# Single blocks at the opening of two passes, a moved product, and one tile in another PSUM bank, in a two-layer decode kernel with its gradients

## The chip, the cores and the metric

The kernel runs on one core of one Trainium2 chip. The metric is the device time of one execution in microseconds (us); the number of a kernel is the median of its runs. Lower is better.

## The reference

One token (S = 1, D = 1024) goes through four blocks: attention over a cache of 65536 positions (32 query heads, 4 groups of cached heads, 128 wide), a feed-forward block (3584 wide, squared ReLU), then the same two with the same weights again. The outputs are the result and the gradients of it (for a given grad_out) by x, both caches, and all weights and biases.

```
def A(x, k_cache, v_cache, wq, wo):          # caches: (1, 4, 65536, 128)
    q = (x @ wq) as (32 heads, 128); k, v repeated 8 times over the heads
    p = softmax(q k^T * 128**-0.5)
    return (p v) @ wo
def B(x, w1, b1, w2, b2):
    return relu(x @ w1 + b1)**2 @ w2 + b2
x = x + A(layernorm(x));  x = x + B(layernorm(x))
x = x + A(layernorm(x));  x = x + B(layernorm(x))
out, vjp = jax.vjp(...);  return out, *vjp(grad_out)
```

All tensors are bfloat16. Each cache is 64 MB; the gradients of the caches are as large.

## The kernel before

The caches don't fit on the chip, so they are streamed from memory four times. Pass 1 is the first attention forward, pass 2 the second attention forward, pass 3 the backward pass of the second attention as far as the gradient of q (attn_bwd3), pass 4 the rest of both backward passes with the cache gradients (attn_bwd4). Between them stand dense stages for the weights. In the code the passes are p = 0 to 3.

**Items and blocks.** A pass walks over 256 items. An item is eight columns of 128 positions of one group; 64 items are a group, four items are a block (1 MB of K or V; 64 blocks of each). Each item runs through some stages with fixed lags: in pass 2 the transpose of K (kT, lag 0), the scores (kS, 2) and the V products (v8, 36); in pass 3 the transpose of V (vT, 0), the products with dO (vS, 2) and the products with K (k8, 13). After the stages of a step, a background queue does one step of work for another group: in pass 2 the query of the next group (g_q, reads wq), in pass 3 its dO and its row sums of dO o (g_dO, reads wo). These generators count steps, with some steps in which they only wait for their load. bg.need(g) finishes what is left of them before the group's first item. by_group says at which step they begin: the second group's at n // 4 = 16 of 64, the others as far into the group before theirs.

**Granules.** The arena holds 20 granules of 1 MB. Eight of them become planes that keep the softmax numerators of two layers, so in pass 3 twelve are left for everything that streams. kv8 loads a block on first touch: either a pair of blocks in two adjacent granules (take_pair; one request of 2 MB, line 370), or a single one (Slot; 1 MB, line 365). The set KV["halves"] names the blocks that are always loaded singly: the last eight of the order in which the pass touches its blocks, and at the beginning of passes 2 to 4 the first ten. Pass 4 never loads pairs (NOW["pairs"] is false there). take_pair chooses the pair whose later granule came free first, take_one the granule that has been free longest, both by the count of steps at which the plan gives granules back, not by measured time. Some blocks are kept from one pass to the next: eight K blocks into pass 2, seven V blocks into pass 3, most of them already transposed in place.

**Order.** In passes 1 to 3 and in the second dense stage the order of instructions on TensorE, VectorE and ScalarE is the order of the program (manual_schedule). In pass 4 it is made by the framework's scheduler. All loads are issued on SyncE, in program order; SyncE waits only for the granule of the load at its head, so it runs ahead of the computation. Stores are issued on GpSimd.

**The row sums.** The gradient of the scores needs dO v^T minus the row sums of dO o. Its accumulator ps_dp holds 64 columns x 8 heads (pass 3; a unit of eight items) or 32 x 16 (pass 4; a block). The unit begins with one product of the constant sel2 with ndt, the negated row sums (as two bfloat16 parts) spread to the unit's width; it starts the accumulation and writes all of it. Then come 64 (32) products of V blocks with the padded dO (dOpad, DOB). ndt is made on VectorE in vS at the group's first item, after dO_finish, right behind dOpad.

**The second dense stage.** Between passes 2 and 3 the feed-forward block runs forward and backward over w1 in seven chunks. Per chunk: ch_fwd (32 products and two VectorE steps, giving dhb), ch_bwd of the chunk before, ch_spread (four products spread dhb over the partitions, ScalarE copies them to wvb), ch_turn (four groups of transposes of w1; ScalarE copies three of them, VectorE one) and ch_dots (VectorE products of w1 with wvb). The PSUM tiles of ch_spread and of ch_turn come from one ring of three buffers, ps_tr. The tag acc has one buffer; passes 2 and 3 accumulate their outputs there.

Of the kernel before, what the change touches and what calls it, by code (L numbers as in the profile page):

```python
# [11 lines left out]
F32 = mybir.dt.float32  # L12
# [4 lines left out]
P = 128  # L17
# [3 lines left out]
def kernel(  # L21
# [35 lines left out]
    J = 32  # L57
# [3 lines left out]
    HB = 64  # L61
# [3 lines left out]
    R2, R4 = 2 * R, 4 * R  # L65
# [16 lines left out]
    PS = {}  # L82
# [5 lines left out]
    def ps_tr(shape=None, dtype=BF):  # L88
        return PS["pool"].tile(shape or [P, 8, P], dtype, name="ps_tr", tag="tr", bufs=2 if PS["pass4"] else 3)

    def ps_sc(shape, dtype=F32):
        return PS["pool"].tile(shape, dtype, name="ps_sc", tag="sc", bufs=1 if PS["pass4"] else 2)
# [4 lines left out]
    def ps_acc(shape):  # L97
        return PS["pool"].tile(shape, F32, name="ps_acc", tag="acc", bufs=1)
# [251 lines left out]
    KV = {"have": {}, "keep": set(), "halves": set(), "turn": None, "turned": set()}  # L350
# [74 lines left out]
    def start_pass(p):  # L425
        KV["keep"] = plan_keep(p)
        KV["turned"] = KV.get("next", set())
        KV["next"] = set()
        KV["turn"] = {0: "k", 2: "v"}.get(p)
        NOW["pairs"] = p < 3  # L430
        KV["halves"] = set(TOUCH[p][-8:] + (TOUCH[p][:10] if p else []))

    def f_cols(ap, nb):
        return ap[:, bass.ds(512 * (nb // 4) + nb % 4, P, step=4)]
# [342 lines left out]
    class Background:  # L777
# [35 lines left out]
        def by_group(self, p, gen):  # L813

            order = list(dict.fromkeys(g for g, _ in ITEMS[p]))
            n = len(ITEMS[p]) // G
            for k, g in enumerate(order[1:]):
                self.later.append((k * n + 8 if PS["pass4"] and k else k * n + n // 4, gen(g), g))

        def drain(self):  # L820
            while self.later:
# [376 lines left out]
    def attn_bwd3(p, L, on_group, bg, end=()):  # L1198
        st = ExitStack()
        dspool = st.enter_context(tc.tile_pool(name="b3_ds", bufs=2))  # L1200
        items = ITEMS[p]
        dOpad = vec.tile([P, G, 8, R], BF, name="dOpad")
        nc.vector.memset(dOpad[:], 0.0)
        state = {}
        gfirst = {g: next(c8 for gg, c8 in items if gg == g) for g in range(G)}
        glast = {g: [c8 for gg, c8 in items if gg == g][-1] for g in range(G)}

        def vT(g, c8):
            bg.need(g)
            vb8 = kv8("v", g, c8)  # L1210
            if is_turned("v", g, c8):
                state[("vt", g, c8)] = vb8
            else:
                pt = ps_tr()
                for i in range(8):
                    nc.tensor.transpose(pt[:, i, :], vb8[:, i, :], ident_b[:, :])  # L1216
                kv_done("v", g, c8)
                vt = turned_to("v", g, c8, vb8)
                evac(vt[:, :, :], pt[:, :, :], kind="kta" if c8 % HB // 8 in ACT_VT else "kt")
                state[("vt", g, c8)] = vt  # L1220

        def vS(g, c8):
            if c8 == gfirst[g]:
                nc.vector.tensor_copy(out=dOpad[:, g, 0, :], in_=L["dOT"][:, gsl(g)])
                ndt = dspool.tile([64, HB, R], BF, name="ndt", tag="ndt")
                nc.vector.tensor_copy(out=ndt[:, :, :], in_=L["nd2"][:, gsl(g)].unsqueeze(1).to_broadcast([64, HB, R]))
                state["ndt"] = ndt
            vt = state.pop(("vt", g, c8))
            for i in range(8):
                s = (c8 + i) % HB  # L1230
                if s == 0:
                    state["ps_dp"] = ps_sc([P, HB, R])
                    nc.tensor.matmul(state["ps_dp"][:, :, :].rearrange("p c r -> p (c r)"), lhsT=sel2[:, :],
                                     rhs=state["ndt"][:, :, :].rearrange("o c r -> o (c r)"), start=True, stop=False)
                w = min(8, HB - s)
                nc.tensor.matmul(state["ps_dp"][:, s:s + w, :].rearrange("p a b -> p (a b)"), lhsT=vt[:, i, :],
                                 rhs=dOpad[:, g, 0:w, :].rearrange("p a b -> p (a b)"), start=False, stop=(s == HB - 1))
            if is_turned("v", g, c8):
                kv_done("v", g, c8)
            if (c8 + 8) % HB == 0:  # L1240
                c0 = c8 + 8 - HB
                ps_dp = state["ps_dp"]

                def ds():
                    dsT = dspool.tile([P, HB, R], BF, name="dsT", tag="dsT")
                    nc.vector.tensor_tensor(out=dsT[:, :, :], in0=ps_dp[:, :, :], in1=E(1, g, c0, HB), op=ALU.mult)
                    add_load(dve=0.7)
                    state[("ds", g, c0 // HB)] = dsT
                after(1, ds)

        def k8(g, c8):
            kb8 = kv8("k", g, c8)
            dsT = state[("ds", g, c8 // HB)]
            if c8 % SU == 0:
                state["ps_dq"] = ps_acc([P, 8, R])
            ps_dq = state["ps_dq"]
            for i in range(8):
                c = c8 + i
                s = c % HB
                w = min(8, HB - s)  # L1260
                nc.tensor.matmul(ps_dq[:, 0:w, :].rearrange("p a b -> p (a b)"), lhsT=kb8[:, i, :],  # L1261
                                 rhs=dsT[:, s:s + w, :].rearrange("p a b -> p (a b)"),
                                 start=(c % SU == 0), stop=(c % SU == SU - 1), skip_group_check=True)
            kv_done("k", g, c8)
            if (c8 + 8) % SU == 0:
                su = c8 // SU

                def fold():
                    fold_dq(L, g, su, ps_dq[:, 0, :], gfirst[g] // SU == su, glast[g] // SU == su, dspool)
                    if glast[g] // SU == su:  # L1270
                        on_group(g)
                first_at(1, fold)

        start_pass(p)
        with tc.manual_schedule(engines=ORDERED):
            pipeline(items, [(vT, 0), (vS, TLEAD), (k8, B3_LAG)], bg, end)
        st.close()


    def attn_bwd4(p, La, Lb, on_group, bg, stack, end=()):  # L1280
# [5 lines left out]
        state = {}  # L1286
# [69 lines left out]
        def vS(g, c8):  # L1356
            if c8 == gfirst[g]:
                g_setup(g)
            vt = state.pop(("vt", g, c8))
            for i in range(8):  # L1360
                s = (c8 + i) % J
                if s == 0:
                    state["ps_dp"] = ps_sc([P, J, R2])
                    nc.tensor.matmul(state["ps_dp"][:, :, :].rearrange("p c r -> p (c r)"), lhsT=sel2[:, :],
                                     rhs=state["ndt"][:, :].unsqueeze(1).to_broadcast([64, J, R2]), start=True, stop=False)
                w = min(4, J - s)
                nc.tensor.matmul(state["ps_dp"][:, s:s + w, :].rearrange("p a b -> p (a b)"), lhsT=vt[:, i, :],  # L1367
                                 rhs=DOB[:, g, 0:w, :].rearrange("p a b -> p (a b)"), start=False, stop=(s == J - 1))
            if is_turned("v", g, c8):
                kv_done("v", g, c8)  # L1370
                if c8 % J == J - 8 and nexts:
                    NOW["newest"] = True
                    kv8(*nexts.popleft())
                    NOW["newest"] = False
                    NOW["ring"] = not nexts
            if (c8 + 8) % J == 0:
                c0 = c8 + 8 - J
                ps_dp = state["ps_dp"]
                if g == items[0][0]:
                    if c8 == J - 8 + items[0][1]:  # L1380
                        state["Xs"] = Slot("xs")
                    X = state["Xs"].t.rearrange("p (n j r) -> p n j r", j=J, r=R2)[:, c0 // J % 8, :, :]
                else:
                    X = dspool.tile([P, J, R2], BF, name="X", tag="X", bufs=3)
                nc.vector.tensor_tensor(out=split2(X[:, :, :]), in0=split2(ps_dp[:, :, :]), in1=E2(g, c0, J), op=ALU.mult)
                add_load(dve=0.13 + J * R2 * 0.00105)
                state[("X", g, c0 // J)] = X
# [310 lines left out]

    def ch_spread(s):

        pg = ps_tr([P, 512], F32)
        for j in range(4):
            nc.tensor.matmul(pg[:, j * P:(j + 1) * P], lhsT=dhb[:, 4 * s + j:4 * s + j + 1].to_broadcast([P, P]), rhs=ident_b[:, :],
                             start=True, stop=True)
        nc.scalar.copy(out=wvb[:, s % 2, :].rearrange("q (p j) -> q p j", j=4), in_=pg[:, 0:512].rearrange("q (j p) -> q p j", j=4))
# [232 lines left out]
```

## Time and profile before

| | |
|---|---|
| median of 3 runs | 1951.35 us (1949.32 to 1955.88) |
| profiled execution | 1954.17 us, span 1952.4 us |
| mean granted TensorE clock | 0.916 |
| TensorE products busy | 1592.5 us (82%) |
| VectorE busy | 1172.5 us (60%) |
| ScalarE busy | 1044.6 us (54%) |
| DMA | 787.63 MB, mean 403 GB/s |
| read from memory, written | 617.62 MB, 165.69 MB |
| K and V loads of 2 MB | 169 requests |
| K and V loads of 1 MB | 152 requests |

The profile is one execution, 1.8 us longer than its span. In it PE is TensorE, DVE VectorE, ACT ScalarE, POOL GpSimd, SP SyncE; a q behind the name (SPq) is the engine's instruction queue. L1236 is line 1236 of the kernel. A row of the timeline has start, duration, engine, line, operation, output <- input, and in brackets how long the engine had been idle and what ended that. A row of the view by stretches has the busy time of each engine with its instructions, the granted clock, the DMA share (mean busy share of 16 DMA engines; it can pass 1 a little) and GB/s. A row of waits has who waited for whom: total us, times, longest.

### The profile page before, as it was taken

The page shows a single profiled execution, that of the slowest core. Times are in us where ns is not written, and L with a number is a line of the kernel's source. Part 1 is how long each engine was busy: PE and PEld are TensorE (multiplying, and loading weights), DVE is VectorE, ACT ScalarE, POOL GpSimd, SP SyncE. Part 2 cuts the span into 40 slices and gives each one's busy share as a digit, 9 for nine tenths or more (in the row PEclk, how much of TensorE's full clock was granted, in tenths as well). Part 3 has the DMA queues.
Part 4 walks back from the last instruction along what each step waited for, and adds up shares of the span by engine and source line. Part 5 has one row for each costly group of instructions (what it writes and reads, how often), then busy time and mean ns, then how long its engine had stood idle before and what let it go on. Part 6 is the DMA issues. An engine that isn't in the chain of part 4 may idle for free. (4 is left out here: it accounts for less than half of the span.)

```text
span 1952.4 us, 66978 instructions
## 1 busy us (share of the span) xinstructions
PE 1592.5 (82%) x30199; PEld 1304.0 (67%) x30199; DVE 1172.5 (60%) x2453; ACT 1044.6 (54%) x1617; POOL 141.8 (7%) x321
## 2 busy tenths in 40 slices
PE   6878788688878888877787888889987987787977
PEld 6868778587777777777776885555554554454544
DVE  5645555255545555545464576867875886676866
ACT  3434334254334446435363455766875785676765
POOL 0000000000000000000000001211211211121211
PEclk9999899699899999999899999988996998898997
DMA  9999999999999999899999988999999999899998
GB/s 395 426 426 427 426 428 413 397 398 424 429 425 428 427 423 304 333 425 428 427 423 418 408 309 302 416 405 406 424 423 420 401 424 412 355 423 392 424 422 318
DMA packets 105997, 787.63 MB, mean 403 GB/s; under 512 B 9312, under 2 KB 16494, under 8 KB 42094
## 3 DMA queue, kind: packets, MB, share of 16 engines
q1 hardware_dynamic: 81630, 617.65, 76.8%
q0 software_dynamic: 24080, 165.70, 20.4%
q8 instruction: 236, 3.87, 0.7%
q14 instruction: 51, 0.42, 0.1%
HBM read 617.62 MB, written 165.69 MB: 401 GB/s over the span
## 5 line engine op out<-in xcount | busy, mean ns | idle before, releaser
L164 DVE COPY kt<-ps_tr 128x1024 bf16<-128x1024 bf16 x724 | 497.0, 689 | 438.2 <-PE ps_tr L1024 244.6
L161 ACT CAST arena<-ps_gg 128x1024 bf16<-128x1024 f32 x457 | 444.5, 1011 | 194.7 <-PE ps_gg L1408 145.1
L1024 PE MATMUL ps_tr<-ident_b,arena 128*128 128x128 bf16 x3840 | 309.2, 225 | 32.3 <-DMA arena<-in_A_k_cache_dram 21.0
L164 DVE CAST arena<-ps_gg 128x1024 bf16<-128x1024 f32 (+2 forms) x186 | 222.4, 1196 | 86.4 <-PE ps_gg L1408 41.6
L161 ACT COPY kt<-ps_tr 128x1024 bf16<-128x1024 bf16 x164 | 171.3, 1052 | 186.5 <-PE ps_tr L1216 112.0
L1024 PEld LDWEIGHTS <-arena 128*128 128x128 bf16 x3840 | 233.5, 101 | 39.8 <-DMA arena<-in_A_k_cache_dram 23.4
L1126 PE MATMUL ps_acc<-arena 128*128 128x64 bf16 (+4 forms) x4096 | 205.8, 196 | 64.5 <-DMA arena<-in_A_v_cache_dram 51.9
L1408 PE MATMUL ps_gg<-GG,xt 64*128 64x512 bf16 x1024 | 212.8, 413 | 41.8 <-DVE arena L164 29.1
L1126 PEld LDWEIGHTS <-arena 128*128 128x128 bf16 x4096 | 159.9, 100 | 70.1 <-DMA arena<-in_A_v_cache_dram 55.6
L1336 PE MATMUL ps_tr<-ident_b,arena 128*128 128x128 bf16 x1824 | 178.5, 233 | 32.5 <-DMA arena<-in_A_v_cache_dram 30.5
L1107 ACT ACTIVATE arena<-S_sb,L_negm 128x128 bf16<-128x128 f32 x256 | 165.7, 1005 | 63.7 <-DVE L_negm L1092 63.7
L1042 PE MATMUL ps_sc<-L_qpad,kt 128*128 128x64 bf16 (+7 forms) x3584 | 183.5, 194 | 17.8 <-ACT kt L161 8.9
L1216 PE MATMUL ps_tr<-ident_b,arena 128*128 128x128 bf16 x1920 | 155.4, 227 | 42.6 <-DMA arena<-in_A_v_cache_dram 41.8
L1336 PEld LDWEIGHTS <-arena 128*128 128x128 bf16 x1824 | 118.0, 104 | 88.6 <-issue 54.0
L1042 PEld LDWEIGHTS <-kt 128*128 128x128 bf16 x3584 | 153.0, 100 | 22.6 <-ACT kt L161 11.8
L1216 PEld LDWEIGHTS <-arena 128*128 128x128 bf16 x1920 | 117.9, 102 | 46.6 <-DMA arena<-in_A_v_cache_dram 44.4
L1439 PEld LDWEIGHTS <-arena 128*128 128x128 bf16 x2048 | 95.1, 102 | 61.9 <-issue 42.2
L1107 ACT ACTIVATION_READ_ACCUMULATOR arena<-S_sb,L_negm 128x1 f32 x256 | 128.4, 502 | 0.0
L1408 PEld LDWEIGHTS <-xt 64*128 64x128 bf16 x1024 | 64.6, 94 | 87.9 <-issue 49.4
L587 ACT ACTIVATE mv_t<-mv_t 128x1024 bf16<-128x1024 bf16 x96 | 102.0, 1064 | 36.1 <-DVE mv_t L598 36.0
L1261 PE MATMUL ps_acc<-dsT,arena 128*128 128x64 bf16 (+7 forms) x2048 | 102.9, 194 | 16.1 <-DMA arena<-in_A_k_cache_dram 13.2
L1367 PE MATMUL ps_sc<-DOB,kt 128*128 128x64 bf16 (+3 forms) x1824 | 113.3, 198 | 0.0
(317 smaller groups left out, 2156.9 us busy)
## 6 DMA issues: line engine op xcount, KB each, us to landing
arena<-in_A_k_cache_dram SPq DMA_DIRECT2D x86, 2048.0 KB, 21.3
arena<-in_A_v_cache_dram SPq DMA_DIRECT2D x83, 2048.0 KB, 21.2
out_dram<-arena POOLq DMA_DIRECT2D x149, 1024.0 KB, 17.0
arena<-in_A_v_cache_dram SPq DMA_DIRECT2D x76, 1024.0 KB, 13.7
arena<-in_A_k_cache_dram SPq DMA_DIRECT2D x76, 1024.0 KB, 14.8
arena<-in_A_wo_dram SPq DMA_DIRECT2D x22, 1024.0 KB, 13.9
arena<-in_B_w_dram SPq DMA_DIRECT2D x21, 1024.0 KB, 9.1
arena<-in_A_wq_dram SPq DMA_DIRECT2D x18, 1024.0 KB, 13.6
```

The source lines that it names most:

```text
L161: nc.scalar.copy(out=out, in_=in_)
L164: nc.vector.tensor_copy(out=out, in_=in_)
L587: nc.scalar.activation(out=t[:, :], in_=t[:, :], func=ACTF.Copy, accum_out=y[:, kc:kc + 1])
L1024: nc.tensor.transpose(pt[:, i, :], kb8[:, i, :], ident_b[:, :])
L1042: nc.tensor.matmul(state["ps_s"][:, s:s + w, :].rearrange("p a b -> p (a b)"), lhsT=kt[:, i, :], rhs=L["qpad"][:, g, 0:w, :].rearrange("p ...
L1107: nc.scalar.activation(out=E(p, g, c0, SU)[:, :, h], in_=S[:, h, :], func=ACTF.Exp, bias=L["negm"][:, g, su, h:h + 1], scale=SCALE, accum_ ...
L1126: nc.tensor.matmul(ps_o[:, 0:w, :], lhsT=vb8[:, i, :], rhs=E(p, g, c, w), start=(c % SU == 0), stop=(c % SU == SU - 1), skip_group_check=True)
L1216: nc.tensor.transpose(pt[:, i, :], vb8[:, i, :], ident_b[:, :])
L1261: nc.tensor.matmul(ps_dq[:, 0:w, :].rearrange("p a b -> p (a b)"), lhsT=kb8[:, i, :], rhs=dsT[:, s:s + w, :].rearrange("p a b -> p (a b)") ...
L1336: nc.tensor.transpose(pt[:, i, :], vb8[:, i, :], ident_b[:, :])
L1367: nc.tensor.matmul(state["ps_dp"][:, s:s + w, :].rearrange("p a b -> p (a b)"), lhsT=vt[:, i, :], rhs=DOB[:, g, 0:w, :].rearrange("p a b - ...
L1408: nc.tensor.matmul(pg[:, 512 * h:512 * h + 512], lhsT=xt[64 * h:64 * h + 64, j1 // 8 + m, :], rhs=gg[64 * h:64 * h + 64, :, :].rearrange(" ...
```

## The change

Four things change. KV["halves"] takes the first 18 blocks of passes 2 and 3 in place of 10 (the same edit covers pass 4, which loads singly anyway). The background work of the second group in these two passes begins at step 32 in place of 16. In passes 3 and 4, in the first unit of each group, the product with ndt comes after the unit's last V product, and the first V product starts the accumulation; the other units stay as they are. ch_spread takes its PSUM tile from ps_acc in place of ps_tr. Of the moved product the edit in pass 3 is shown; that in attn_bwd4 is the same with J, R2 and DOB.

```
-        KV["halves"] = set(TOUCH[p][-8:] + (TOUCH[p][:10] if p else []))
+        KV["halves"] = set(TOUCH[p][-8:] + (TOUCH[p][:18] if p else []))
...
-                self.later.append((k * n + 8 if PS["pass4"] and k else k * n + n // 4, gen(g), g))
+                self.later.append((k * n + 8 if PS["pass4"] and k else k * n + n // (2 if p in (1, 2) and k == 0 else 4), gen(g), g))
...
                 if s == 0:
                     state["ps_dp"] = ps_sc([P, HB, R])
+                late = c8 + i - s == gfirst[g]
+                w = min(8, HB - s)
+
+                def delta(first):
                     nc.tensor.matmul(state["ps_dp"][:, :, :].rearrange("p c r -> p (c r)"), lhsT=sel2[:, :],
-                                     rhs=state["ndt"][:, :, :].rearrange("o c r -> o (c r)"), start=True, stop=False)
-                w = min(8, HB - s)
+                                     rhs=state["ndt"][:, :, :].rearrange("o c r -> o (c r)"), start=first, stop=not first,
+                                     skip_group_check=True)
+                if s == 0 and not late:
+                    delta(True)
                 nc.tensor.matmul(state["ps_dp"][:, s:s + w, :].rearrange("p a b -> p (a b)"), lhsT=vt[:, i, :],
-                                 rhs=dOpad[:, g, 0:w, :].rearrange("p a b -> p (a b)"), start=False, stop=(s == HB - 1))
+                                 rhs=dOpad[:, g, 0:w, :].rearrange("p a b -> p (a b)"), start=late and s == 0,
+                                 stop=(s == HB - 1) and not late, skip_group_check=True)
+                if s == HB - 1 and late:
+                    delta(False)
...
-        pg = ps_tr([P, 512], F32)
+        pg = ps_acc([P, 512])
```

More of the change, by code (lines that the diff above doesn't have):

```diff
@@ L1363, in vS, with delta @@
                     state["ps_dp"] = ps_sc([P, J, R2])
+                late = c8 + i - s == gfirst[g]
+                w = min(4, J - s)
+                def delta(first):
                     nc.tensor.matmul(state["ps_dp"][:, :, :].rearrange("p c r -> p (c r)"), lhsT=sel2[:, :],
-                                     rhs=state["ndt"][:, :].unsqueeze(1).to_broadcast([64, J, R2]), start=True, stop=False)
-                w = min(4, J - s)
+                                     rhs=state["ndt"][:, :].unsqueeze(1).to_broadcast([64, J, R2]), start=first, stop=not first,
+                                     skip_group_check=True)
+                if s == 0 and not late:
+                    delta(True)
                 nc.tensor.matmul(state["ps_dp"][:, s:s + w, :].rearrange("p a b -> p (a b)"), lhsT=vt[:, i, :],
-                                 rhs=DOB[:, g, 0:w, :].rearrange("p a b -> p (a b)"), start=False, stop=(s == J - 1))
+                                 rhs=DOB[:, g, 0:w, :].rearrange("p a b -> p (a b)"), start=late and s == 0,
+                                 stop=(s == J - 1) and not late, skip_group_check=True)
+                if s == J - 1 and late:
+                    delta(False)
             if is_turned("v", g, c8):
```

## The prediction

> **What bounds the kernel now.** I read the page's head first, then the stretches by stage, then the opening of each pass in steps of 4 us, and last the SP queue there.
>
> ```profile
> span 1952.4 us, 66978 instructions
> ...
> GB/s 395 426 426 427 426 428 413 397 398 424 429 425 428 427 423 304 333 425 428 427 423 418 408 309 302 416 405 406 424 423 420 401 424 412 355 423 392 424 422 318
> ```
>
> Most of the 40 slices move some 425 GB/s, whatever the engines do. What costs time is therefore a stretch in which too little is asked for; the slices near 300 GB/s are such places. The stages, with the DMA share and GB/s as the last two columns:
>
> ```profile
> 413.00:735.00 322.00, 262.32 (x6246) 249.94 (x6244) 171.88 (x394) 142.48 (x346) 0.00 (x0) 0.95 1.00 422
> ...
> 785.00:805.00 20.00, 18.77 (x468) 17.29 (x469) 10.64 (x22) 10.08 (x14) 0.00 (x0) 1.00 0.60 231
> 805.00:1114.00 309.00, 243.38 (x5466) 226.14 (x5463) 149.68 (x291) 136.70 (x185) 0.00 (x0) 0.93 1.01 424
> ```
>
> Passes 2 (413 to 735) and 3 (805 to 1114) run at a share of 1.00 and 1.01: there a faster engine wins nothing. The first 20 us of pass 3 are at 0.60, although PE is busy for 18.8 of them. In smaller steps, pass 2's opening in the first two rows and pass 3's in the others:
>
> ```profile
> 412.00:416.00 4.00, 3.51 (x103) 3.40 (x101) 0.36 (x2) 0.19 (x1) 0.00 (x0) 0.79 0.68 287
> 416.00:420.00 4.00, 2.68 (x91) 2.55 (x88) 2.01 (x6) 0.98 (x2) 0.00 (x0) 1.00 0.80 279
> ...
> 792.00:796.00 4.00, 4.00 (x104) 4.00 (x104) 2.37 (x4) 2.00 (x3) 0.00 (x0) 1.00 0.83 340
> 796.00:800.00 4.00, 4.00 (x104) 3.35 (x100) 1.57 (x3) 0.97 (x3) 0.00 (x0) 1.00 0.04 14
> 800.00:804.00 4.00, 4.00 (x127) 3.72 (x124) 2.64 (x5) 3.18 (x6) 0.00 (x0) 1.00 0.29 61
> 804.00:808.00 4.00, 1.46 (x39) 1.34 (x36) 2.10 (x5) 1.37 (x3) 0.00 (x0) 1.00 0.93 385
> ```
>
> The missing shares times 4 us are 1.28 + 0.80 = 2.1 us in pass 2, and 0.68 + 3.84 + 2.84 + 0.28 = 7.6 us in pass 3. Since the rest of each pass is at a share of 1, a microsecond of DMA idleness here is a microsecond at the end, and one saved is saved. The SP queue (start, time, line, request) says what was missing:
>
> ```profile
> 415.79 0.33 SPq L370 DMA_DIRECT2D arena<-in_A_v_cache_dram  x1
> ...
> 788.58 0.33 SPq L462 DMA_DIRECT2D arena<-in_A_wo_dram  x1
> 789.70 0.33 SPq L365 DMA_DIRECT2D arena<-in_A_v_cache_dram  x1
> 802.32 0.33 SPq L370 DMA_DIRECT2D arena<-in_A_k_cache_dram  x1
> ```
>
> and the view of SP's waits from 760 to 850 why:
>
> ```profile
> SPq L370 <- PE ps_sc L1236: 12.6, 2, 12.2
> ```
>
> L365 is a single block (1 MB), L370 a pair (2 MB). After the single V block at 789.70 nothing is asked for until 802.32, when the first K pair goes out; SP stood 12.2 us before it, until a product of L1236 gave its granule back. A pair needs two adjacent granules, and take_pair counts it free only when the later one is. Granules did come free meanwhile:
>
> ```profile
> 792.18 0.61 PE L1216 MATMUL ps_tr<-ident_b,arena 128*128 128x128 bf16 x8
> ...
> 795.37 0.61 PE L1216 MATMUL ps_tr<-ident_b,arena 128*128 128x128 bf16 x8
> ...
> 796.51 0.51 PE L1261 MATMUL ps_acc<-dsT,arena 128*128 128x64 bf16 x8
> ...
> 800.07 0.39 PE L1236 MATMUL ps_sc<-dOpad,arena 128*128 128x64 bf16 x8
> ...
> 801.93 0.35 PE L1236 MATMUL ps_sc<-dOpad,arena 128*128 128x64 bf16 x8
> ...
> 810.19 0.61 PE L1261 MATMUL ps_acc<-dsT,arena 128*128 128x64 bf16 x8 [4.73 <-DMA arena<-in_A_k_cache_dram]
> ```
>
> The row at 792.18 is the last transpose of V block 2 (three of the seven resident V blocks are transposed only here, twelve groups of eight products), so its granule is free at 792.18 + 0.61 = 792.8; V block 3 at 796.0 (the twelfth); K block 0 (fourth group of L1261) at 797.0; V block 4 at 800.5; V block 5 at 802.3, where the pair goes. At 810.19 PE has waited 4.73 us for that pair.
>
> **The change part by part.**
>
> *18 single blocks in pass 3.* By the order of first touch, ten singles end with V block 6; eighteen reach V block 10, so K blocks 4 to 7 and V blocks 8 to 11 become single: four pairs become eight requests. The queue was K0, wo, K1, K2, K3, wo, V7, pair K4. It becomes K0 to K3, V7, K4, V8, wo, K5, V9, K6, because the second group's wo load moves from step 16 to step 32. The seven granules that were free by 789.70 now carry seven K and V blocks, the next (792.8) wo, 796.0 carries K5, 797.0 V9, 800.5 at the latest K6. 1 MB at 424 GB/s takes 2.5 us. DMA had work until 795.3 (0.83 of the 4 us from 792), hence wo fills it to 797.8, K5 to 800.3, V9 to 802.8, K6 to 805.3: no gap. I take the whole 7.6 us; the bounds are 7.6 and, if the gap only moves (rival 2), 2.6. The compute that follows reads in the order in which SP asks, so a later wo arrives before the later blocks; nothing new waits on it. With the load move the second group's other instructions: nine small products on PE, ten copies and sums on ACT, eight products on DVE, and the short chain to its row sums; its 25 steps from step 32 end at 57, and the group needs them at 64. That costs nothing, covered by the share of 1.01; if the 7 steps of slack were gone, the rest would run at once at step 64 under the same cover. POOL's queue is passed by nothing.
>
> *The same in pass 2.* K8 and K9 are single before and after; the pairs from V0, K10, V2 and K12 become eight singles, and the second group's wq load with its 64 one-column products moves behind K8. The gap ends with the pair at 415.79. A single needs one granule, and those of the dense stage's last slabs come free one by one before. I take 2.1 us (bounds 0 and 2.1).
>
> Does a smaller request cost more? Eight single V blocks that pass 2 ends with, a window in which they move, and four 1 MB wo requests of the dense stage's end, into a queue with little in it (time to landing, min/median/max):
>
> ```profile
> 704.36 15.86 SPq L365 DMA_DIRECT2D arena<-in_A_v_cache_dram  x8
> ...
> 720.00:724.00 4.00, 3.78 (x109) 3.61 (x106) 2.04 (x5) 3.71 (x10) 0.00 (x0) 1.00 1.02 424
> ...
> DMA to landing us min/median/max: 5.0/5.4/5.8
> ```
>
> Queued singles move 424 GB/s, like pairs: 0 us for eight more requests a kernel (four a pass). Almost alone, one takes 5.4 us instead of 2.5; that is rival 4. The Trainium skill, "DMA: Bandwidth & Descriptors", section "Measured (HBM→SBUF, 128 partitions, SWDGE, issued from GpSimd)", speaks against the change: it gives 341 GB/s for a 1 MB request and a fixed 2.0 us for each; by it the eight would add an estimated 16 us and the kernel would be near 1957 us. The row at 720, 424 GB/s of single requests, disagrees as long as requests queue.
>
> *w1 spread in another bank.* PE and ACT in one chunk of the dense stage, and L1694's named waits (us, times):
>
> ```profile
> 763.06 0.44 PE L1694 MATMUL ps_tr<-ident_b,arena 128*128 128x128 bf16 x5 [0.16 <-ACT wvb L1705]
> 763.65 0.44 PE L1694 MATMUL ps_tr<-ident_b,arena 128*128 128x128 bf16 x5 [0.15 <-ACT wt L1696]
> ...
> 762.90 1.89 ACT L1696 COPY wt<-ps_tr 128x640 bf16<-128x640 bf16 x3
> ...
>   ACT wt L1696: 0.9, 5
>   ACT wvb L1705: 0.5, 3
> ```
>
> ch_turn's third transpose group waits 0.16 us for the copy of the spread, since it is fourth in a ring of three buffers. With the spread in the free acc bank this wait goes (0.5 us in all). But then the fourth group reuses the first group's buffer, which ACT copies from 762.90 on, after the spread's copy: exactly what the group at 763.65 waits for today. It starts at 763.65 again. I take 0; the bounds are 0 and 0.5 + 0.9 = 1.4 us, both waits. Between pass 2's last V product and pass 3's first K product nobody else holds acc, so nothing below zero. The Trainium skill, "Perfetto Trace Analysis", section "Optimization Strategy", reads a gap that repeats as a sign of too few buffers; by it the change would win up to those 1.4 us. The row at 763.65 says that the copy's order on ACT holds it, not the number of banks.
>
> *Row sums last in a group's first unit.*
>
> ```profile
> 784.56 0.17 DVE L1224 CAST dOpad<-L_dOT 128x8 bf16<-128x8 f32 x1
> ...
> 786.23 0.39 PE L1233 MATMUL ps_sc<-ndt,sel 64*128 64x512 bf16 x1 [1.30 <-DVE ndt L1226]
> ...
> 859.44 0.37 PE L1233 MATMUL ps_sc<-ndt,sel 64*128 64x512 bf16 x1 [1.71 <-DVE ndt L1226]
> ...
> 1183.42 0.17 DVE L1297 CAST DOB<-L_dOT 128x8 bf16<-128x8 f32 x1
> ...
> 1185.43 0.39 PE L1364 MATMUL ps_sc<-ndt,sel 64*128 64x512 bf16 x1
> ...
> 1182.00:1186.00 4.00, 3.18 (x67) 2.24 (x64) 2.59 (x19) 1.44 (x3) 1.16 (x4) 1.00 0.12 49
> 1186.00:1190.00 4.00, 3.26 (x72) 2.15 (x68) 2.72 (x15) 1.57 (x4) 0.62 (x1) 1.00 0.52 156
> ```
>
> In pass 3 the first product waited 1.30 us for ndt; dOpad is ready at 784.7, so the unit can open at about 785.0 and the 0.39 us product follows five microseconds later, when ndt (there at 786.2) is no longer late. At the other three groups (859.44: 1.71 us) dOpad comes just before ndt on DVE, and the share is 1. What hides both is DMA: after the first part there is no gap left that 1.3 us could shorten. I take 0, bounds 0 and 1.3. In pass 4 DOB is ready at 1183.6, the product with ndt starts at 1185.43, and DMA idles 3.5 us and 1.9 us in the two windows, because each V block's end releases the next load. The first unit could open up to 1.6 us earlier, but other products on PE fill that time. I take 0.5, bounds 1.6 and, through a new order of instructions, rival 5's loss.
>
> **Sum.** 7.6 + 2.1 + 0 + 0 + 0.5 = 10.2 us. The profiled execution took 1954.2 us (span 1952.4 and 1.8 around it), 2.8 over the median 1951.35; less 10.2 it is 1944.0, the median 1941.1 us.
>
> **The rivals.**
> 1. Forecast, 1941.1 us.
> 2. The gap moves to the first pair after the singles (K8): it again waits 12.2 us, with three more requests (7.4 us) queued before it, so 4.8 us idle remain; 5.1 us gained, 1946.3 us. For it: granules are as scattered as before. Against: nine of twelve are free by then.
> 3. Granules, not pairs, are the limit, or the time is given back in the next dense stage: 0 to 2.1 gained, 1949 to 1951 us. Against: the five granules above.
> 4. Slower: requests don't queue, and each extra one costs what the lone wo cost, 5.4 - 2.5 = 2.9 us; eight are 23.2 us, 1964 us. It decides from 1.3 us a request. Against: 424 GB/s.
> 5. Slower: pass 4, whose order isn't written out by hand, is laid out anew around the moved products. Its stalls have this size:
>
> ```profile
> 1675.00:1700.00 25.00, 13.46 (x160) 9.03 (x159) 11.50 (x18) 10.21 (x15) 2.15 (x5) 0.66 0.77 307
> ```
>
> 25 x 0.23 = 5.8 us each. Two more eat the gain (1952.6), three give 1958 us. Against: only 4 of 64 units change.
>
> **How the numbers follow.** A measurement of this kernel tells 0.3% (5.9 us) from no change. Forecast 0.62, rival 2 0.16, rival 3 0.10, rival 5 0.08, rival 4 0.04. Faster by over 0.3%: 0.62; within: 0.16 + 0.10 = 0.26; slower: 0.12. The lower end is the sum of the upper bounds, 7.6 + 2.1 + 1.4 + 1.3 + 1.6 = 14.0: 1937 us; the upper takes in rivals 2 and 3: 1951.5 us. Rivals 4 and 5 are left out.
>
> **What would show it.** In the profile after: SP asks for a single block every 1 to 4 us from 789 to 803, and the DMA share there is above 0.95; the wait of PE at 810 is gone; around 414 the share is above 0.95; the fourth transpose group of each chunk still waits for ACT's wt and the chunks take as long; pass 4 opens some 10 us earlier. I am wrong if a gap of over 3 us stands before the first pair of pass 3, if the share falls below 0.97 while singles are loaded, or if pass 4 is longer than before by over 3 us.

## The result, and the profile after

| | before | after |
|---|---|---|
| median, first comparison | 1955.65 us (7 runs) | 1944.60 us (7 runs) |
| ratio after / before | | 0.9948, 95% interval 0.993 to 0.9966 |
| the same kernels once more | 1953.94 us (21 runs) | 1942.84 us (5 runs), 0.9944 (0.9932 to 0.9957) |
| profiled execution, span | 1954.17, 1952.4 us | 1939.92, 1938.1 us |
| bytes moved, mean rate | 787.63 MB, 403 GB/s | 787.63 MB, 406 GB/s |

The changed kernel takes about 10.5 us less (10.2 by the first ratio, with an interval of 6.6 to 13.7; 10.9 by the second); 10.2 was forecast. The median of before over all its later runs is 3 to 5 us above the 1951.35 us of its first three, so the differences and ratios are compared below, not the absolute 1941.1 us. The sum is right; the parts are not all, and that is what the experiments are about.

The opening of pass 3, first by SP's queue of the kernel after (start, time, line, request; L365 is a single block, L370 a pair, L462 a dense load):

```profile
785.40 0.33 SPq L365 DMA_DIRECT2D arena<-in_A_v_cache_dram  x1
787.97 0.33 SPq L365 DMA_DIRECT2D arena<-in_A_k_cache_dram  x1
...
792.62 0.33 SPq L462 DMA_DIRECT2D arena<-in_A_wo_dram  x1
...
799.15 0.33 SPq L365 DMA_DIRECT2D arena<-in_A_k_cache_dram  x1
...
807.63 0.33 SPq L365 DMA_DIRECT2D arena<-in_A_v_cache_dram  x1
816.28 0.33 SPq L370 DMA_DIRECT2D arena<-in_A_k_cache_dram  x1
```

then by its stretches (busy time of PE, PEld, DVE, ACT and POOL, granted clock, DMA share, GB/s):

```profile
796.00:800.00 4.00, 3.97 (x126) 3.60 (x123) 1.20 (x2) 0.00 (x0) 0.00 (x0) 1.00 1.01 416
800.00:804.00 4.00, 1.75 (x52) 1.48 (x48) 0.36 (x1) 0.00 (x0) 0.00 (x0) 1.00 1.01 418
...
812.00:816.00 4.00, 4.00 (x86) 3.36 (x83) 1.98 (x3) 2.15 (x4) 0.00 (x0) 1.00 0.95 397
816.00:820.00 4.00, 4.00 (x112) 4.00 (x108) 2.73 (x5) 3.21 (x5) 0.00 (x0) 1.00 0.83 279
```

Where before nothing was asked for from 789.70 to 802.32 and the share fell to 0.04, requests now go out in steps of 0.4 to 3.9 us up to 807.63 and the share is 1.01. The gap before the first pair has become small: 0.05 + 0.17 of 4 us, 0.9 us of idle DMA.

**A ruler for the openings.** Marks such as "pass 3 began at" scatter by some 2 us between profiles, more than most parts of this change are worth. The rate in a fixed stretch that begins at the same instruction leaves out what came before it: in pass 2 from 14 us before its first score products to 12 us after, in pass 3 from 2 us before its row sums (L953) to 50 after, in pass 4 from 2 us before its row sums to 46 after. Before, and after, in this order:

```profile
399.74:425.74 26.00, 20.62 (x554) 19.75 (x552) 9.29 (x32) 11.79 (x20) 0.61 (x13) 0.93 0.95 376
782.70:834.70 52.00, 41.76 (x967) 39.00 (x964) 25.20 (x61) 22.92 (x32) 0.00 (x0) 0.93 0.83 339
1181.56:1229.56 48.00, 40.99 (x638) 26.63 (x635) 33.49 (x77) 27.98 (x33) 9.80 (x20) 0.93 0.79 296
```

```profile
399.60:425.60 26.00, 21.56 (x551) 20.56 (x551) 9.48 (x31) 11.56 (x19) 0.61 (x13) 0.93 0.98 393
783.78:835.78 52.00, 46.47 (x1113) 43.27 (x1110) 26.71 (x55) 24.69 (x34) 0.00 (x0) 0.97 0.96 394
1175.95:1223.95 48.00, 43.64 (x695) 28.79 (x692) 36.07 (x81) 30.57 (x36) 10.22 (x20) 0.96 0.84 319
```

Bytes that were moved early need not be moved later, so the difference in GB/s times the stretch, divided by the 424 GB/s of a full stretch, is time saved: here 17 x 26 / 424 = 1.0 us, 55 x 52 / 424 = 6.7 us and 23 x 48 / 424 = 2.6 us. The whole bytes are the same, so what the ruler shows can only be given back by idle DMA later. All kernels below were measured with it. A single profile still scatters, in the table by up to 17 GB/s or 2.1 us in pass 3, 19 GB/s or 2.2 us in pass 4 and 17 GB/s or 1.0 us in pass 2, so the means are compared; rows with one or two profiles are good to a microsecond or two only:

| GB/s in the stretch of | kernels without the part | kernels with it | worth |
|---|---|---|---|
| pass 3: singles and late product | 339, 340, 336 | 394, 404, 389, 390, 387, 388, 394, 401 | 6.8 us |
| pass 3: late product without singles | 339, 340, 336 | 345 | 0.8 us |
| pass 3: singles without late product | 339, 340, 336 | 363, 381 | 3.0 and 5.2 us |
| pass 2: singles, deferred wq as a pair | 376, 376, 370, 377, 380, 386 | 393, 393, 388, 391, 376, 384 | 0.6 us |
| pass 2: singles, deferred wq as singles | the same | 416, 416 | 2.4 us |
| pass 4: late product | 296, 299, 286, 302, 302, 299 | 319, 307, 326, 326, 320, 320, 311, 319 | 2.4 us |

The worth is from the means, as above. The whole change is 6.8 + 0.6 + 2.4 = 9.8 us by it. In every run the singles of a pass and its later wq or wo load go together; none tells the two apart.

### The profile page after: what moved, and what is told of

It is laid out like the page before. It is cut to its first block, busy times and chain, and to the rows that moved or that the text cites. A ratio compares the mean times of both kernels' runs of the same rounds, so it can differ in the third digit from the quotient of the medians.

```text
span 1938.1 us, 66986 instructions
## 1 busy us (share of the span) xinstructions
PE 1585.2 (82%) x30199; PEld 1301.4 (67%) x30199; DVE 1170.3 (60%) x2453; ACT 1044.9 (54%) x1617; POOL 142.2 (7%) x321
## 2 busy tenths in 40 slices
DMA packets 107149, 787.63 MB, mean 406 GB/s; under 512 B 9440, under 2 KB 16622, under 8 KB 42222
## 5 line engine op out<-in xcount | busy, mean ns | idle before, releaser
L1042 PE MATMUL ps_sc<-L_qpad,kt 128*128 128x64 bf16 (+7 forms) x3584 | 183.0, 194 | 16.3 <-issue 8.3
L1270 PE MATMUL ps_acc<-dsT,arena 128*128 128x64 bf16 (+7 forms) x2048 | 103.1, 194 | 11.3 <-DMA arena<-in_A_k_cache_dram 7.8
```

The costliest lines, as they stand in the source:

```text
L1042: nc.tensor.matmul(state["ps_s"][:, s:s + w, :].rearrange("p a b -> p (a b)"), lhsT=kt[:, i, :], rhs=L["qpad"][:, g, 0:w, :].rearrange("p ...
```

## The experiments

Each kernel was timed in five rounds against the kernel before. A is the prediction with its terms; B takes the parts as the marks of the one profile after suggest them (pass 3 shorter by 6.7 us, pass 4 by 8.7, pass 2 not at all). Other letters are explained where they stand.

### Pass 3's opening alone

```
-        KV["halves"] = set(TOUCH[p][-8:] + (TOUCH[p][:10] if p else []))
+        KV["halves"] = set(TOUCH[p][-8:] + (TOUCH[p][:18 if p == 2 else 10] if p else []))
...
-   k * n + n // 4, gen(g), g))
+   k * n + n // (2 if p == 2 and k == 0 else 4), gen(g), g))
```

> The kernel before with the 18 single blocks and the later wo load in pass 3 alone. Theory A (the forecast's terms): the idle DMA time of pass 3's opening is the main gain, so 7.6 us faster, and the DMA share from 792 to 808 us is near 1. Theory B (the two profiles' marks: pass 3 with the dense stage behind it is 6.7 us shorter, pass 4 is 8.7 us shorter): 5 to 7 us faster, all of it before pass 4 opens. Rival C (the gap only moves to the first pair): 3 us or less.

Measured: 1950.63 against 1956.11 us, ratio 0.9978 (0.9965 to 0.9991): 4.3 us less (1.8 to 6.8), below A's 7.6 and at the lower edge of B's 5 to 7. The ruler gives 3.0 us. PE's timeline, SP's waits from 787 to 797 and two stretches show what lacks:

```profile
787.59 0.23 PE L953 MATMUL ps_mv<-dlt_prod,ones_f 128*33 128x8 f32 x2 [0.46 <-DVE dlt_prod L950]
789.12 0.61 PE L1233 MATMUL ps_sc<-ndt,sel 64*128 64x512 bf16 x1 [1.29 <-DVE ndt L1226]
789.66 1.03 PE L1236 MATMUL ps_sc<-dOpad,arena 128*128 128x64 bf16 x16
```

```profile
SPq L365 <- PE ps_sc L1236: 5.4, 1, 5.4
```

```profile
790.00:792.00 2.00, 2.00 (x32) 2.00 (x30) 0.00 (x0) 0.42 (x1) 0.00 (x0) 0.50 0.99 406
792.00:794.00 2.00, 2.00 (x45) 2.00 (x43) 0.69 (x1) 1.19 (x2) 0.00 (x0) 0.90 0.72 238
```

PE waits 1.29 us for the row sums at the pass's start. The first single that has no free granule (K4) needs V block 0's, which PE gives back only after that. SP stands 5.4 us, and the share falls to 0.72 in a stretch that the sum had counted as full. Here PE was also at half clock after its wait (0.50 in the first of these rows), which made the delay longer.

### Pass 2's opening alone

The same two edits with p == 1.

> The kernel before with the 18 single blocks and the later wq load in pass 2 alone. Theory A: 2.1 us faster, the DMA share from 412 to 420 us near 1. Theory B: 0 to 1 us, since the changed kernel's mark at the end of pass 2 stands 0.25 us later than that of the kernel before although its share at 412 was 1.07: what is saved there is lost in the windows before (0.91 and 0.84 from 404 to 412).

Measured: 1954.77 against 1956.11 us, ratio 0.9996 (0.9983 to 1.0009): 0.8 us less, from 3.3 less to 1.8 more. Too little to tell A's 2.1 from nothing by the runs; the ruler says 0.6 us over all kernels that have it. SP's queue and the stretches of the kernel after, which opens pass 2 in the same order, show why (before, four single wq requests stood here, all sent by 400.3, and no pair):

```profile
395.97 2.61 SPq L365 DMA_DIRECT2D arena<-in_A_k_cache_dram  x1
407.11 0.37 SPq L462 DMA_DIRECT2D arena<-in_A_wq_dram  x1
407.53 0.57 SPq L365 DMA_DIRECT2D arena<-in_A_k_cache_dram  x1
```

```profile
404.00:408.00 4.00, 3.92 (x99) 3.74 (x95) 0.65 (x7) 3.46 (x4) 0.00 (x0) 1.00 0.91 369
408.00:412.00 4.00, 2.48 (x57) 2.31 (x58) 1.64 (x10) 0.45 (x2) 0.61 (x13) 0.93 0.84 300
412.00:416.00 4.00, 3.51 (x86) 3.40 (x84) 0.36 (x2) 0.00 (x0) 0.00 (x0) 0.64 1.07 432
416.00:420.00 4.00, 2.68 (x92) 2.55 (x88) 1.71 (x4) 1.17 (x2) 0.00 (x0) 1.00 1.01 422
```

The gap at 412 to 420 is gone, but the deferred wq load now comes as one request of 2 MB. It waits for two adjacent granules at SP's head, from the end of the request before at 398.6 to 407.1, with the singles behind it: 0.36 + 0.64 = 1.0 us of idle DMA, earlier than the 2.1 us that went.

### The late product in pass 4 alone

The edit of the whole change in attn_bwd4, nothing else.

> The kernel before with the row sums added last in pass 4 alone. Theory A: 0.5 us faster, from the first unit, and the rest of pass 4 as before. Theory B: 4 to 9 us faster, because the scheduler lays pass 4 out in another order throughout, and the changed kernel's pass 4 was 8.7 us shorter in the profile; the pass opens at the same time as in the kernel before.

Measured: 1954.11 against 1956.11 us, ratio 0.9987 (0.9973 to 1.0): 2.5 us less, from 5.3 to 0. A's 0.5 lies in that, most of B's 4 to 9 does not. What the edit does is seen below.

### All but the late product in pass 4

The whole change with the old attn_bwd4.

> The changed kernel without the moved product in pass 4 (all else as changed). Theory A: 9.7 us faster than the kernel before. Theory B: 5 to 7 us faster, pass 4 as long as in the kernel before (its order of instructions on TensorE is that of the kernel before).

Measured: 1945.71 against 1956.11 us, ratio 0.9948 (0.9931 to 0.9966), the whole change's own ratio. That is 10.2 us less (6.7 to 13.5); B's 5 to 7 lie almost wholly outside. The pass 4 of 760.1 us in the profile after against 768.8 before was mostly the spread of single profiles: by the same marks the kernels without the late product took 763.3 to 768.8 us for pass 4, those with it and no other edit there 759.9 to 765.1, 3.4 us less on the mean.

### The late product in pass 3 alone, and with the singles

For the first, only the edit in attn_bwd3 as in the diff of the change; for the second, that and pass 3's opening.

> Only the late product of pass 3 is put into the kernel before. A (the prediction: the product of the sums lies under the DMA engines): 1956, the same as before. D (the singles and the late product of pass 3 work together: the product keeps TensorE from standing still for the 1.29 us for ndt at the pass's start, so the first granule of V is given back earlier, but only a request that waits for that one granule can use it): 0 to 2 us less, 1954 to 1956, since without singles the first request of the pass that waits is for wo. G (the late product is worth its 5 us by itself, at 16 group starts of 0.3 us): 1951.

> Pass 3 opens with 18 singles and its first load of wo at half of group 0, and the late product of pass 3 is put in; pass 2, the spread of w1 and pass 4 stay as before. A (terms of the prediction that add up, with what the opening alone measured): 4.3 us less, 1952, and its first request of the pass goes out as late as with the opening alone, 5.4 us after the pass's first instruction on TensorE. D (together): 8 to 10 us less, 1946 to 1948; that request goes out 2 to 3 us after the first instruction, and the DMA engines idle under 3 us in the opening. G (late product alone 5 us, singles 4.3): 1946.5 too, and is told from D by the late product alone.

Measured: alone 1954.16 against 1953.94 us, ratio 0.9998 (0.9987 to 1.0009), so nothing, and G falls; together 1948.43 us, ratio 0.9965 (0.9948 to 0.9982), 6.8 us less (3.5 to 10.2). That is less than D's 8 to 10 and 2.5 us more than the singles alone, though the two intervals overlap. The mechanism that D named is there, in the timeline and waits of the second kernel:

```profile
786.75 0.23 PE L953 MATMUL ps_mv<-dlt_prod,ones_f 128*33 128x8 f32 x2 [0.46 <-DVE dlt_prod L950]
786.92 0.64 PE L1242 MATMUL ps_sc<-dOpad,arena 128*128 128x64 bf16 x16
...
791.52 0.39 PE L1237 MATMUL ps_sc<-ndt,sel 64*128 64x512 bf16 x1
```

```profile
SPq L365 <- PE ps_sc L1242: 3.2, 2, 2.2
```

The V products begin 0.17 us after the row sums' product, where they began 2.07 us after it in the kernel with the opening alone, the product with ndt comes last, and SP's longest wait for V products is 2.2 us instead of 5.4. In the kernel with the late product alone wo goes out 2.2 us after the row sums' product too (3.9 before), but the first pair still only 16.8 us after it (17.6 before): the gap in front of the pair takes back half of what the earlier granule wins.

### The whole change without the late product in pass 3

> The whole change but the late product of pass 3. A (the prediction: that product costs and gains nothing): 0.994 to 0.995 of before, as the whole change. D (the singles of pass 3 reach their worth only with it): 2 to 4 us above the whole change, 0.996 to 0.9965 of before; the first request of pass 3 that waits goes out 4 to 6 us after the pass's first instruction on TensorE instead of 2.2.

Measured: 1945.76 against 1955.73 us, ratio 0.995 (0.9931 to 0.9969), 9.8 us less. D's 2 to 4 us are not seen: the whole change has 0.9944 to 0.9948, at most 1.2 us better by these medians, though the interval doesn't exclude them. Its timeline, waits and stretches have the step between the two:

```profile
788.31 0.39 PE L1233 MATMUL ps_sc<-ndt,sel 64*128 64x512 bf16 x1 [1.30 <-DVE ndt L1226]
```

```profile
SPq L365 <- PE ps_sc L1236: 4.7, 2, 3.9
```

```profile
790.00:792.00 2.00, 2.00 (x52) 2.00 (x49) 0.90 (x2) 1.65 (x2) 0.00 (x0) 1.00 1.01 422
```

PE's wait is as long as in the kernel with pass 3's opening alone, but the clock stays at 1.00 and SP stands 3.9 us instead of 5.4. The late product brings this first request forward by 3.9 - 2.2 = 1.7 us and those behind it as well: counted from the row sums' product, wo goes out at 6.8 us in the whole change and at 8.1 here, K5 at 10.0 and 11.3. What that is worth shows in the 8 us that begin 10 us after that product, here and in the whole change:

```profile
796.78:804.78 8.00, 6.35 (x189) 5.92 (x187) 1.63 (x3) 1.01 (x1) 0.00 (x0) 1.00 1.00 360
```

```profile
795.78:803.78 8.00, 5.72 (x177) 5.20 (x173) 1.52 (x3) 0.14 (x1) 0.00 (x0) 1.00 1.02 421
```

The share is full in both, but here the engines move 360 GB/s and there 421. Over the same 8 us all eight kernels with both edits move 415 to 421 GB/s, the one with the opening alone 341 at a share of 0.97. The 61 GB/s are worth 61 x 8 / 424 = 1.2 us. The late product is worth 1 to 2 us beside the singles (1.6 by the ruler, 394 against 381 GB/s, from one profile each). The 2.5 us above, against the kernel in whose profile the clock fell, may be more for that reason; this is not shown.

### The whole change without its part in pass 2, and the whole change again

> The whole change but its part in pass 2 (10 singles there, the load of wq at a quarter, as before). A (the prediction: the opening of pass 2 is worth 2.1 us): 1946.5 to 1947, 2 us above the whole change beside it. E (the idle time only moved, because the deferred load of wq now comes as one request of two granules): 0 to 0.8 above the whole change.

> The whole change once more, beside the others on the same chip. A: 0.9948 of before as measured, about 10 us less. By the profile of the whole change its pass 4 took 760.1 us against 768.8 before; if that shortening comes from the late product of pass 4, this profile has 759 to 762 again (theory J); if it was the spread of one profile, 765 to 768 (theory N, as the kernel with all but that product had 767.7).

Measured: without pass 2's part 1945.23 us, ratio 0.9961 (0.9947 to 0.9974); the whole change 1942.84 us, 0.9944 (0.9932 to 0.9957); before 1953.94 us for both. The difference of 2.4 us speaks for A's 2.1, the 0.8 us alone for E; the intervals hold both, and the runs don't settle it. Pass 4 of the whole change took 764.3 us in this profile, between J and N. The rates tell more, and SP's waits in pass 4's opening of the kernels before and after:

```profile
SPq L462 <- PE ps_sc L1367: 18.6, 1, 18.6
```

```profile
SPq L462 <- PE ps_sc L1382: 14.2, 1, 14.2
```

SP stands with a wo load at its head until the V products of a block give a granule back. The wait is 17.2 to 18.7 us in the six kernels without the late product and 13.0 to 16.1 in the seven with it (leaving out the one below whose wo comes later). By its end wo goes out 27.9 to 29.4 us after the row sums' product in the six and 22.8 to 26.0 us in the seven. The first V products begin 0.48 us after the row sums' product, where they began 2.2 us after it before, and the product with ndt follows:

```profile
1177.95 0.23 PE L953 MATMUL ps_mv<-dlt_prod,ones_f 128*33 128x8 f32 x2 [0.46 <-DVE dlt_prod L950]
1178.43 1.07 PE L1382 MATMUL ps_sc<-DOB,arena 128*128 128x64 bf16 x32 [0.25 <-DVE negd L956]
1179.56 0.37 PE L1377 MATMUL ps_sc<-ndt,sel 64*128 64x512 bf16 x1
```

But these are not the products that let wo go. Those are the last eight of the seventh block, 28.9 us after the row sums' product in the kernel before and 23.5 in the one after:

```profile
1205.79 0.61 PE L1486 MATMUL ps_gg<-rowb,rowa 2*128 2x512 bf16 x2 [3.65 <-DVE arena L164]
...
1212.47 0.37 PE L1367 MATMUL ps_sc<-DOB,arena 128*128 128x64 bf16 x8
```

```profile
1182.24 0.66 PE L1457 MATMUL ps_acc<-arena 128*128 128x64 bf16 x17
...
1198.36 0.39 PE L1504 MATMUL ps_gg<-rowb,rowa 2*128 2x512 bf16 x2 [1.70 <-DVE arena L164]
...
1201.46 0.55 PE L1382 MATMUL ps_sc<-DOB,arena 128*128 128x64 bf16 x8
```

The first V products moved by 1.7 us, these by 5.4. In between the order itself is another: in all eight kernels with the late product 17 products into ps_acc stand 4.3 us after the row sums' product, in the six without it the first such product comes 16.3 us after it. TensorE's longest wait on the way, for a copy on VectorE, is 1.1 to 2.5 us in the eight and 3.1 to 4.0 in the six. So the framework's scheduler laid out the opening of pass 4 anew around the moved product. How much of the gain is the earlier first block and how much the new order, no run separates.

### The deferred wq load in single granules, twice

The whole change, and

```
-            if ks and flat and NOW["wide"] and not odd_one():
+            if ks and flat and NOW["wide"] and not odd_one() and not (KV.get("p") == 1 and NOW["i"] < 48):
```

with KV["p"] set to p in start_pass. It bars pairs for dense loads in the first 48 steps of pass 2.

> The whole change, but the deferred load of wq in pass 2 asks for single granules instead of a pair. E (the pair holds SP's head from 398.6 to 407 and so leaves about 1 us of DMA time empty): the empty time at 406 to 410 goes, 0.5 to 1 us less than the whole change. F (the pair does not cost anything that lasts, the room is taken from later loads): the same as the whole change.

> The whole change with single granules for the deferred load of wq in pass 2, once more, for the size of its lead over the whole change. E (the pair took back what the singles of pass 2 gave): pass 2 ends in the profile at 744.0 to 745.3, where the six kernels with the deferred pair or without the change in pass 2 that ended earliest had 745.7 to 746.6, and the ratio to before is 0.992 to 0.9945. F (the first run of it was a draw of the spread): pass 2 ends at 746 to 747, ratio 0.9945 to 0.996.

Measured: 1942.26 against 1955.73 us, ratio 0.993 (0.9908 to 0.9953), and 1942.04 against 1955.36 us, 0.9933 (0.9917 to 0.9948). The opening of pass 2 by the ruler and SP's queue, in the first of the two:

```profile
399.11:425.11 26.00, 20.69 (x558) 19.52 (x554) 9.82 (x34) 12.43 (x21) 0.61 (x13) 1.00 1.03 416
```

```profile
399.11 0.37 SPq L463 DMA_DIRECT2D arena<-in_A_wq_dram  x1
402.09 0.34 SPq L365 DMA_DIRECT2D arena<-in_A_k_cache_dram  x1
...
412.65 0.38 SPq L463 DMA_DIRECT2D arena<-in_A_wq_dram  x1
```

The rate is 416 GB/s in both, 2.4 us over the kernels without any change in pass 2, and the stretch has no idle time left. Pass 2 ended at 744.69 and 745.47 in the profiles, against 745.75 to 748.80 in the others; the second missed the 745.3 that was set for it by 0.2 us. E holds: the pair had taken back most of what the singles gave. This kernel has the best ratio of all, 13.1 to 13.7 us under the kernel before; its lead over the whole change, 2 to 3 us, is seen in the stretch and in both ratios, but the intervals overlap.

### The later wo load in pass 4 too

```
-  n // (2 if p in (1, 2) and k == 0 else 4)
+  n // (2 if p in (1, 2, 3) and k == 0 else 4)
```

> The whole change, and pass 4 too asks for its first load of wo at half of group 0 instead of a quarter. P (in pass 4's opening SP stands for 13 to 18 us with that wo at its head while the DMA engines lie idle for 4 to 6 us): 3 to 5 us less than the whole change, 1936 to 1940 where the whole change has 1941 to 1945. Q (the room is what lacks, not the order of the requests: granules in pass 4 come free only as the products end): the same within 1 us, the wait is then for a V or K block. R (wo comes too late and stalls the sums of group 1): slower than the whole change by 2 to 6 us.

Measured: 1952.01 against 1955.73 us, ratio 0.9985 (0.9968 to 1.0002), about 8 us slower than the whole change. The opening, and SP's longest wait there:

```profile
1175.89:1223.89 48.00, 43.65 (x707) 28.90 (x704) 36.27 (x81) 29.94 (x35) 10.87 (x21) 0.96 0.84 319
```

```profile
SPq L365 <- PE ps_sc L1382: 14.1, 1, 14.1
```

The rate is the 319 GB/s of the whole change, and the wait of 14 us is there, now for a V block: P's gain didn't come, and Q is right about the opening, there is no granule for any request. The loss lies behind it (412 GB/s in the next 344 us where the whole change has 417, 392 against 400 in the rest). R named a loss of this size, but its cause, a stall of group 1's sums, was not shown; that the scheduler lays out pass 4 anew around the later load would do as well. This stays open.

## Why the prediction was right, and where its steps were not

**The bound holds.** An empty microsecond of the DMA engines in an opening is one at the end, as far as the sum over the openings goes: 9.8 us by the ruler, 10.2 and 10.9 us by the runs. A loss behind an opening is not seen by the ruler, as the later wo load in pass 4 shows.

**Pass 3, forecast 7.6 us: 6.8, and not by the singles alone.** The list of free granules was right, with its order of requests and its 2.5 us each. But the sum asked only whether the DMA engines are busy. The granules that PE gives back in the opening follow PE's start, so with PE 1.7 us later the requests go out 1.3 us later, and the rate falls at a full share (360 GB/s above). The step that failed is "after the first part there is no gap left that 1.3 us could shorten": the late product, sized at 0, carries 1 to 2 us of these 6.8, about its upper bound of 1.3. Rival 2 is there in small: SP asks for nothing for 8.7 us before the first pair, and 0.9 us of DMA are idle in place of 4.8. (Its sum was a little off: 7.6 - 4.8 is 2.8 and not 2.6, so 5.4 us would have been gained and not 5.1.)

**Pass 2, forecast 2.1 us: 0.6.** The step that failed is "those of the dense stage's last slabs come free one by one": true, but the load that moves behind K8 takes a pair as soon as the pass allows pairs, and that was not in the list of what is moved. With singles there too, the opening gives 2.4 us, so the size of the gap had been right. The marks at pass 2's end say much the same, with their scatter: 746.6 us on the mean without the change in pass 2 and with the deferred pair, 745.1 with the singles.

**The bank, forecast 0.** In the kernel after the third group's wait is gone and the fourth waits as before and longer:

```profile
764.74 0.44 PE L1712 MATMUL ps_tr<-ident_b,arena 128*128 128x128 bf16 x5 [0.47 <-ACT wt L1714]
```

```profile
PE ps_tr L1712 <- ACT wt L1714: 2.1, 5, 0.5
```

2.1 us in all, where both waits together had 1.4. The fourth group starts 1.71 us after the spread's first product in both kernels (763.65 and 764.74, with the spread at 761.94 and 763.03), so the order of the copies on ACT holds it, as the prediction said. The spreads of two chunks were copied at 763.51 and 767.26, 3.75 us apart, as far as before (758.67 and 762.42). TensorE's wait is not what sets that time: VectorE's products of ch_dots begin 3.75 us apart too, wait 1.15 us for the spread's copy each time, and the next spread needs the dhb that VectorE makes behind them. No run moves the bank alone. From pass 2's end to pass 3's start the six kernels without the move took 38.7 to 40.2 us, the eight with it 38.7 to 41.4, so a gain or loss under a microsecond would not be seen. The gap that repeats, which by the Trainium skill can mean a lack of buffers ("Perfetto Trace Analysis", section "Optimization Strategy"), is not one here: the added buffer moved it by one group.

**Pass 4, forecast 0.5 us: about 2.4.** The step that failed is the one from 1.6 to 0.5, "other products on PE fill that time". They do, but in another order: the granule on which SP stands with wo comes free 4.7 us earlier on the mean, and the prediction had counted a new order only as a loss. The first block itself opened 1.7 us earlier, about as said; the upper bound of 1.6 for the whole was too low. Runs alone don't settle the size: alone it gave 2.5 us (0 to 5.3), taken out of the whole change nothing. Rival 5's mechanism, a new order of instructions, is there, but its loss is not: the pass is not longer.

**Requests of 1 MB.** Rival 4 falls: the share is 1.01 where only singles are loaded. The rows at 796 and 800 have 416 and 418 GB/s with requests queued. The 341 GB/s that the Trainium skill gives for 1 MB ("DMA: Bandwidth & Descriptors", section "Measured (HBM→SBUF, 128 partitions, SWDGE, issued from GpSimd)") do not bind such requests. The fixed 2.0 us that the prediction named with them stands on the same page of the Trainium skill in another section, "Anatomy of one DMA — SWDGE (gpsimd) path"; eight requests more did not cost 16 us here, the kernel became faster.

So three errors, 0.8 and 1.5 us too much and 1.9 too little, nearly cancel; that the sum came out this close is in part luck. Of the signs named beforehand PE's wait at 810 went (two of 2.25 and 2.63 us stand at 803 and 829 instead, under a full DMA share), and the others came too but two: the share around 414 rose to 1.07, but the idle time stood earlier, at 407 to 410; and pass 4 opened 5.6 us earlier in that profile, not 10 (785.78 against 784.70 at pass 3's start is 1.1 us of that).

## What to carry to other kernels

When transfers are the bound, list for each request which instruction gives back the room it takes, and from when: the moved request has to be in that list with its own size, since one large request at the head of an in-order queue holds back all small ones behind it. A product that waits costs nothing while no request stands on its output; once smaller requests use every granule, the same wait reaches the queue, so an edit that is worth nothing alone can be worth something beside another. Where a scheduler makes the order, look at the order again after a small edit, since one moved product changed it. And compare a fixed stretch after the same instruction: the mean of its rate over six or more profiles resolved about a microsecond, where single profiles scattered by one to two, whole passes by several and runs by two.

## What was not expected of the hardware

A TensorE gap of 1.29 us was followed by a granted clock of 0.50 for some 3 us in the kernel with pass 3's opening alone, and one of 1.30 us by none in the kernel before and in the one without the late product. The Trainium skill, "TensorE: Matmul & The Clock Gate", section "HAM oscillation — how this bites in real kernels", warns of gaps over about 3.4 us; the row at 790.00 shows the drop after a far shorter one. What decides it was not tried.

A full DMA share is not full rate: 360 GB/s at a share of 1.00 in the kernel without the late product in pass 3, where wo and K5 go out 1.3 us later after the pass's start, against 421 at 1.02. That too few queued requests are the reason is argued from SP's times, not shown by a run of its own. One figure doesn't fit it simply: the K and V requests sent in that stretch took longer to land there (medians of 8.8 and 10.2 us) than in the whole change (7.4 and 8.8).
